# A pair's heads 64 partitions apart: scores as float32 products of two 48-row halves in place of three rounded passes over 96 rows

## The chip, the core and the metric

The kernel runs on one core of a Trainium2 chip. A core has a matrix engine (TensorE, PE in the profile, its weight loads PEld), a vector engine (DVE), a scalar engine (ACT), GpSimd (POOL) and an engine that issues transfers (SyncE, SP). The metric is the device time of one execution in microseconds, the median over the runs shown. Lower is better.

## The reference

Two steps follow each other. First a recurrence over 768 time steps, for 4 batches of 8 heads of 48 features: each head holds a 48 x 48 state.

```
for t in range(S):
    cur = einsum('bhd,bhe->bhde', u * k[t], v[t])
    y[t] = einsum('bhd,bhde->bhe', r[t], state + cur)
    state = w[t][..., None] * state + einsum('bhd,bhe->bhde', k[t], v[t])
```

The outputs of the 8 heads side by side are x, 3072 rows of 384. Then a feed-forward: h = x @ w_in (384 x 2048), g = h * cos(h), out = g @ w_out (2048 x 384). The feed-forward weights arrive as 64-bit floats; all else is float32.

## The kernel before, in words

**Chunks.** Time is cut into chunks of 128 steps, 6 per batch, 24 in all (`j`). Two batches run interleaved, so a chunk's predecessor in its batch is `j` - 2; `c` is the chunk's place in its batch. Inside a chunk the recurrence is written as matrix products. Heads are taken in 4 pairs, 2 x 48 = 96 features on 96 partitions.

**Steps of a chunk.** `load` brings one tile `tt` with r, k and the decays, features on partitions; `lr` and `lv` bring r, k and v with time on partitions. `decay` (L184) makes two running products of the decays by scans (L191, L198; `ee` holds one of them), then multiplies r (`r3`, L203) and k (`k3`, L204) by them in place. `split` (L206) prepares the scores' operands. `a0` and `a1` (L243) make the scores of two pairs each, 128 x 128 per head, into a bank `pa`, and a masked copy (L257) puts the part above the diagonal into `asb`, into which `diag` has put the current step's own term. `t` (L259) transposes k3 into `kn`. `s` (L269) makes the new state `sn` from kn and v; `d` (L235) decays the old state into `dd`. `y` (L296) adds the old state's part (`dd` times `r3`, the past) and the chunk's own (`v` times `asb`) in the bank `py`, heads of a pair in the lower and the upper half of the output's partitions, at 0 and 64. `x` writes the result as high and low parts into `xT`.

**Why a split.** A pair's two heads share the 96 rows of a product, so each head's rows of r must be zero where the other head's lie. The first six chunks (`PLAIN`) do that in float32: r times its decays times a 0/1 column `halves`, twice, on DVE (L211, tile `rzf`). The later 18 also round r and k to a shorter format (f32r) that PE takes in one pass, with the rest as a low part: for each head a masked high part on ACT (L125) and a masked low part on DVE (L219), and a high copy of k on DVE (L130) and its low part on POOL (L133). Three products, high-high, high-low and low-high (L254), then make one pair's scores. A float32 product is one instruction in the program and two rows in the trace; an f32r product is one row.

**Feed-forward.** A block is two chunks, 256 rows. A unit is two 128-wide tiles of the hidden layer: `mm1` is 18 products into `ph` (L363), `gate` (L340 to L344, L130, L133) makes g's high and low parts on ACT, DVE and POOL, and `mm2` is 12 products into `acc` (L377). The 16 weight tiles are made from 64-bit floats during the first part of the program by ACT, DVE and POOL (L125, L155, L156, L158, L130, L133).

**What sets the order.** PE's order is written by hand: `START` up to the point where all weights stand, then `PLAN`, four rows per chunk, with one row for each slot. In these tables `y-1` is the step y of the chunk before, `load+2` the load two chunks ahead; `f` and `w` fetch and convert a weight tile. `NEEDS` and `FREES` add steps that must come first. DVE, ACT, POOL and SP run in the order that a scheduler gives them; `EARLY` and `LATER` choose the engine of a step in the two parts (r3 on DVE early, POOL later; k3 on POOL early, DVE later). `BUFS` gives the number of buffers; `tt` has two. Of PSUM's 8 banks, kind "a" has two in turn while the first two blocks run together, then three, for pa, py, pst (the state's products) and pt (the transposes).

## Time and profile before

| What | Value |
|---|---|
| time, median of 3 runs | 598.83 us (598.5 to 600.02) |
| profiled execution, its span | 597.6 us (the page gives no other time of it) |
| PE busy | 528.2 us, 88% |
| DVE busy | 486.7 us, 81% |
| POOL busy | 333.9 us, 56% |
| ACT busy | 268.6 us, 45% |
| mean granted TensorE clock | 0.977 |

A busy time is the time in which at least one instruction of that engine is under way. Matrix products overlap, so their mean durations are longer than the step from one to the next; the step is read from the starts. A group's line names the source line, the engine, the operation, what it writes and reads, its shapes, the count, the busy time and the mean duration, and then the idle time before it with what ended that.

### The profile page before, as it was taken

What the parts mean: (1) busy time and instruction counts of PE and PEld (TensorE: products, weight loads), DVE (VectorE), ACT (ScalarE), POOL (GpSimd) and SP (SyncE); (2) the same over time, 40 slices, a digit from 0 to 9 for tenths busy, and PEclk for the clock granted to TensorE, in tenths of its full rate; (3) what the DMA queues carried; (4) which work ended last, traced back from release to release, by engine and by line L of the source; (5) the groups of instructions that cost most, each with busy time, mean ns of one, the idle gap of its engine ahead of it and who ended that gap; (6) DMA issues with size and microseconds to landing.
All of it is one profiled execution on the core that took longest, in us unless ns stands there. A gap on an engine that the chain in (4) does not pass through costs nothing.

```text
span 597.6 us, 10845 instructions
## 1 busy us (share of the span) xinstructions
PE 528.2 (88%) x4092; PEld 507.8 (85%) x4092; DVE 486.7 (81%) x839; ACT 268.6 (45%) x476; POOL 333.9 (56%) x338
## 2 busy tenths in 40 slices
PE   1633775979999999999999999999999999999995
PEld 0513674869889999999989999999999999999994
DVE  6998899999997897788899678878877977777641
ACT  2353755643635435544334344444345444434541
POOL 3578496554564566575566456657566554722231
PEclk9999887998999999999999999999999999999998
DMA  8629057022143214214513112331242132055000
GB/s 268 227 97 342 7 167 228 1 67 79 33 129 112 61 54 120 55 41 120 133 33 89 53 47 74 94 95 42 78 120 52 44 93 67 8 185 175 32 1 31
DMA packets 23339, 56.07 MB, mean 94 GB/s; under 512 B 4208, under 2 KB 15088, under 8 KB 23280
## 3 DMA queue, kind: packets, MB, share of 16 engines
q1 hardware_dynamic: 23280, 55.31, 30.7%
q8 instruction: 34, 0.56, 0.4%
q14 instruction: 25, 0.20, 0.1%
HBM read 45.86 MB, written 4.72 MB: 85 GB/s over the span
## 4 chain that ended last, share of the span: by engine, by line
PE 67%; DVE 22%; issue 3%; ACT 3%; POOL 2%; DMA 2%; DVEq 0%; SPq 0%
PE ph L363 27%; PE acc L377 27%; PE py L311 6%; PE pa L254 4%; DVE h L155 2%; DVE h L156 2%; DVE rr L344 2%; DVE rr L341 2%; PE pst L275 2%; DVE ee L191 2%; DMA tt<-tr 2%; POOL h L158 2%; DVE gs L130 1%; DVE tt L198 1%; DVE w L133 1%
## 5 line engine op out<-in xcount | busy, mean ns | idle before, releaser
L133 POOL TENSOR_TENSOR gs<-rr,gs 128x256 fp32r<-128x256 f32 x176 | 166.8, 966 | 188.0 <-DVE gs L130 131.0
L363 PE MATMUL ph<-xT,w 128*128 128x256 f32 x1728 | 225.2, 288 | 28.6 <-DVE xT L130 24.0
L363 PEld LDWEIGHTS ph<-xT,w 128*128 128x128 f32 x1728 | 215.1, 195 | 32.9 <-DVE xT L130 24.8
L377 PE MATMUL acc<-w,gs 128*128 128x384 f32 x1152 | 216.2, 337 | 1.6 <-DVE gs L130 1.2
L377 PEld LDWEIGHTS acc<-w,gs 128*128 128x128 f32 x1152 | 196.3, 188 | 3.5 <-DVE gs L130 1.8
L342 ACT ACTIVATE rr<-rr 128x512 f32<-128x512 f32 x96 | 60.7, 633 | 157.4 <-DVE rr L341 157.3
L344 DVE SCALAR_TENSOR_TENSOR rr<-rr,ph 128x512 f32<-128x512 f32 x96 | 65.2, 679 | 42.5 <-ACT rr L343 42.2
L340 ACT ACTIVATE rr<-ph 128x512 int32<-128x512 f32 x96 | 56.9, 593 | 87.0 <-PE ph L363 80.7
L341 DVE SCALAR_TENSOR_TENSOR rr<-rr,ph 128x512 f32<-128x512 int32 x96 | 65.2, 679 | 26.9 <-ACT rr L340 26.8
L343 ACT ACTIVATE rr<-rr 128x512 f32<-128x512 f32 x96 | 60.6, 632 | 2.7
L158 POOL TENSOR_TENSOR h<-h,rd 128x384 int32<-128x384 int32 x32 | 40.3, 1269 | 27.4 <-DVE h L156 26.9
L130 DVE CAST gs<-rr 128x512 fp32r<-128x512 f32 x96 | 45.1, 470 | 5.8 <-PE acc L377 5.5
L311 PE MATMUL py<-asb,v 128*48 128x128 f32 (+1 forms) x384 | 38.5, 291 | 5.0 <-DVE sn L279 3.8
L233 POOL TENSOR_SCALAR_AFFINE_SELECT asb<-cd 128x512 f32<-128x512 f32 x48 | 33.9, 711 | 7.9 <-DVE cd L230 7.3
L191 DVE TENSOR_TENSOR_SCAN ee<-tt,one_e 96x516 f32<-96x516 f32 x24 | 31.9, 1327 | 6.6 <-DMA tt<-tr 6.5
L198 DVE TENSOR_TENSOR_SCAN tt<-tt,inj 96x516 f32<-96x516 f32 x24 | 36.4, 1517 | 0.5
L257 DVE COPY_PREDICATED asb<-mask,pa 128x512 f32<-128x512 uint8 x48 | 35.1, 735 | 0.9 <-POOL asb L233 0.5
L130 ACT CAST w<-h 128x384 fp32r<-128x384 f32 x32 | 16.4, 514 | 40.9 <-POOL h L158 40.9
L203 POOL TENSOR_TENSOR tt<-tt 96x512 f32<-96x512 f32 x18 | 28.0, 1553 | 9.4 <-DVE tt L198 8.1
L311 PEld LDWEIGHTS py<-asb,v 128*48 128x48 f32 (+1 forms) x384 | 25.7, 139 | 7.3 <-issue 5.7
L254 PE MATMUL pa<-rz,ks 96*128 96x256 f32 x216 | 31.5, 282 | 0.1
L133 POOL TENSOR_TENSOR ks<-tt,ks 96x512 fp32r<-96x512 f32 x18 | 25.9, 1439 | 6.0 <-DVE ks L130 6.0
(69 smaller groups left out, 556.3 us busy)
## 6 DMA issues: line engine op xcount, KB each, us to landing
tt<-tr SPq DMA_DIRECT2D x24, 577.9 KB, 4.7
raw<-wts SPq DMA_DIRECT2D x16, 768.0 KB, 7.2
rk<-tn SPq DMA_DIRECT2D x24, 384.0 KB, 3.7
v<-tn SPq DMA_DIRECT2D x24, 192.0 KB, 2.6
out<-ob SPq DMA_DIRECT2D x24, 192.0 KB, 2.3
ww<-w SPq DMA_DIRECT2D x6, 768.0 KB, 4.6
xf<-yf SPq DMA_DIRECT2D x48, 72.0 KB, 2.6
xf<-yf SPq DMA_DIRECT2D x48, 16.0 KB, 1.9
```

The source lines that it names most:

```text
L130: (nc.scalar.copy if E[name] is nc.scalar else E[name].tensor_copy)(out=out, in_=in_)
L133: E[name].tensor_tensor(out=out, in0=full, in1=high.bitcast(F32), op=ALU.subtract)
L158: nc.gpsimd.tensor_tensor(out=h, in0=h, in1=rd, op=ALU.add)
L254: nc.tensor.matmul(out=pa[:, j], lhsT=a["ks"][:, x, p], rhs=a["rz"][:, y, p].rearrange("p h t -> p (h t)"), start=n == 0, stop=n == 2)
L311: nc.tensor.matmul(out=part[0], lhsT=part[n][0], rhs=part[n][1], start=n == 1 or not part[1], stop=n == 2)
L340: nc.scalar.activation(nn, ph, AF.Copy, scale=INV2PI / W_SCALE)
L341: nc.vector.scalar_tensor_tensor(out=rr, in0=nn, scalar=-2.0 * math.pi * W_SCALE, in1=ph, op0=ALU.mult, op1=ALU.add)
L342: nc.scalar.activation(rr, rr, AF.Sin, scale=0.5 / W_SCALE)
L343: nc.scalar.activation(rr, rr, AF.Square)
L344: nc.vector.scalar_tensor_tensor(out=rr, in0=rr, scalar=-0.5, in1=ph, op0=ALU.add, op1=ALU.mult)
L363: nc.tensor.matmul(out=ph[:, fi], lhsT=wgt[u * FU + fi][:, 0, a, kt * 128:(kt + 1) * 128], rhs=xT[:, b, kt], start=n == 0, stop=n == 3 * K ...
L377: nc.tensor.matmul(out=accs[i][j][:, :DM], lhsT=gs[:, a, fi, j * C:(j + 1) * C], rhs=wgt[u * FU + fi][:, 1, b], start=u == 0 and fi == 0 a ...
```

## The change

Features of a pair's two heads now lie on partitions 0 to 47 and 64 to 111 of `tt`, with the rows between filled (r and k with 0, decays with 1), so all tiles by feature have R = 112 partitions in place of 96, and a load brings 112 rows. A head's rows are then the slice `rows(h)`, and:

- The scores take r3 and k3 directly, in float32, one product per head with 48 rows on each side. The step `split`, the tiles rz, rzf and ks, and the plain kind of chunk are gone. r3 is always multiplied in place by its decays.
- `a0` and `a1` are one step `a`: 8 products, the heads in turn, into two banks, one per head of the pairs. `asb` holds one head of all pairs, four buffers in place of three.
- The state and dd keep each head's own 48 x 48 block alone, so they have half the columns. The state's products are one per head, 48 columns each, in the lower and the upper half of the output's partitions; the state is written by one DVE instruction in place of two masked ones.
- In `y` all of the chunk's own products come first, then the past's, one per head with 48 rows each, where the products before had 96 rows.
- `s` moves from the third row of `PLAN` to the first of the next chunk, beside `y`. `START` has no split, `a0`/`a1` become `a`, and the third chunk's load comes later, since `y` now reads r3 from tt in the first chunks too. `dd` has two buffers. Docstrings go.

```diff
-BUFS = dict(tt=2, rk=2, v=2, h=6, rd=3, rr=7, gs=2, asb=3, ahl=2, sn=2, yf=1, past=2, xT=2, rz=1, kn=2, ee=2, dd=1, xf=6, ks=1, cd=1)
+BUFS = dict(tt=2, rk=2, v=2, h=6, rd=3, rr=7, gs=2, asb=4, ahl=2, sn=2, yf=1, past=2, xT=2, kn=2, ee=2, dd=2, xf=6, cd=1)
...
-PLAN = [["y-1 t mm1 split-1 a0 decay+1 mm2"],
+PLAN = [["y-1 s-1 t mm1 decay+1 mm2"],
         ["lv+1 mm1 mm2 load+2"],
-        ["x-3 a1 mm2 diag+1 s d+1 mm1 lr+3"],
+        ["x-3 a mm2 diag+1 d+1 mm1 lr+3"],
         ["mm1 mm2"]]
-START = ["load0 decay0 t0 lr0 lv0 f load1 decay1 f lr1 d0 split0 load2 f lv1 d1 diag0 a00 f w decay2 s0 f",
+START = ["load0 decay0 t0 lr0 lv0 f load1 decay1 f lr1 d0 lv0 f lv1 d1 diag0 a0 f w decay2 s0 f",
...
-        if not (a["plain"] and FUSE):
-            E["r3"].tensor_tensor(out=a["r3"], in0=a["r3"], in1=a["pp"], op=ALU.mult)
+        E["r3"].tensor_tensor(out=a["r3"], in0=a["r3"], in1=a["pp"], op=ALU.mult)
...
+    def rows(h):
+
+        return slice(ROW * h, ROW * h + HD)
...
+        a["dd"] = dd = buf("dd", [R, NP, HD], F32)
+        E["dd"].tensor_tensor(out=dd, in0=states[a["b"]], in1=a["ee"][:, :, 0:1].to_broadcast([R, NP, HD]), op=ALU.mult)
+
+    def att_scores(a):
+
+        pa = [bank("a", [C, NP, C], "pa") for h in range(2)]
+        for p in range(NP):
+            for h in range(2):
+                nc.tensor.matmul(out=pa[h][:, p], lhsT=a["k3"][rows(h), p], rhs=a["r3"][rows(h), p], start=True, stop=True)
+        for h in range(2):
+            nc.vector.copy_predicated(a["asb", h], mask, pa[h])
...
+    def head_cols(p, h):
+
+        at = p * R96 + h * HD
+        return slice(at, at + (ROW if h == 0 else HD))
...
+        for p in range(NP):
+            for h in range(2):
+                m = ROW if h == 0 else HD
+                at = p * R96 + h * HD
+                nc.tensor.matmul(out=pst[ROW * h:ROW * h + m, p * HD:(p + 1) * HD], lhsT=a["kn"][:, head_cols(p, h)],
+                                 rhs=a["v"][:, at:at + HD], start=True, stop=True)
+        new = pst[:R, :NP * HD].rearrange("p (a e) -> p a e", e=HD)
+        if a["c"] == 0:
+            nc.vector.tensor_copy(out=sn, in_=new)
+        else:
+            nc.vector.tensor_tensor(out=sn, in0=new, in1=a["dd"], op=ALU.add)
...
+        past = a["c"] > 0
         for p in range(NP):
-            parts = []
             for h in range(2):
...
+                m = ROW if h == 0 else HD
+                nc.tensor.matmul(out=py[ROW * h:ROW * h + m, p], lhsT=a["v"][:, head_cols(p, h)], rhs=a["asb", h][:, p],
+                                 start=p == 0, stop=not past, skip_group_check=True)
+        for p in range(NP if past else 0):
+            for h in range(2):
+                nc.tensor.matmul(out=py[rows(h), p], lhsT=a["dd"][rows(h), p], rhs=a["r3"][rows(h), p],
+                                 start=False, stop=True, skip_group_check=True)
```

How the order moves, at three places. First PE in the second part of the program, around a chunk's output: before, the end of y (past and own products in turn), the next chunk's transposes, a unit's first half, and the scores of two pairs.

```order
L311 MATMUL py<-tt,dd 64x128
L311 MATMUL py<-tt,dd 48x128
L311 MATMUL py<-asb,v 64x128
L311 MATMUL py<-asb,v 48x128
L264 MATMUL pt<-ident,tt 128x96 x4
L363 MATMUL ph<-xT,w_987 128x256 x9
L363 MATMUL ph<-xT,w_1055 128x256 x9
L254 MATMUL pa<-rz,ks 128x256 x6
L377 MATMUL acc<-w_480,gs 128x384 x2
```

The same place now, first the end of the state's products and the start of y:

```order
L260 MATMUL pst<-v,kn 48x48
L260 MATMUL pst<-v,kn 64x48
L260 MATMUL pst<-v,kn 48x48
L285 MATMUL py<-asb,v 64x128
L285 MATMUL py<-asb,v 48x128
```

and, three pairs of y later:

```order
L285 MATMUL py<-asb,v 64x128
L285 MATMUL py<-asb,v 48x128
L289 MATMUL py<-tt,dd 48x128 x8
L242 MATMUL pt<-ident,tt 128x112 x4
L342 MATMUL ph<-xT,w_398 128x256 x9
L342 MATMUL ph<-xT,w_433 128x256 x9
L356 MATMUL acc<-w_1211,gs 128x384 x2
```

The state's products (pst) now come straight before the chunk's own products (`asb,v`), the past's (`tt,dd`) follow them in one run of eight, and no scores stand behind this unit.

Second, PE at the scores, once a chunk now, between the second products of two units (`acc`):

```order
L356 MATMUL acc<-w_755,gs 128x384 x2
L356 MATMUL acc<-w_815,gs 128x384 x2
L233 MATMUL pa<-tt 128x128 x8
L356 MATMUL acc<-w_881,gs 128x384 x2
L356 MATMUL acc<-w_941,gs 128x384 x2
```

Eight products of 128 columns stand where twice six of 256 stood, and they read tt alone.

Third, DVE with the first chunk. Before:

```order
L198 SCALAR_TENSOR_TENSOR tt<-tt,inj 96x516
L227 TENSOR_TENSOR rk<-rk 128x384
L228 TENSOR_TENSOR rk<-rk,u_sb 128x384
L230 TENSOR_REDUCE cd<-rk 128x8
L105 TENSOR_REDUCE halves<-ident 96x2
L211 SCALAR_TENSOR_TENSOR rzf<-tt,halves 96x4x128
L98 CAST mask<-maskf 128x512
L211 SCALAR_TENSOR_TENSOR rzf<-tt,halves 96x4x128
L155 TENSOR_SCALAR h<-h 128x384
```

Now:

```order
L197 SCALAR_TENSOR_TENSOR tt<-tt,inj 112x516
L206 TENSOR_TENSOR rk<-rk 128x384
L201 TENSOR_TENSOR tt<-tt 112x512
L207 TENSOR_TENSOR rk<-rk,u_sb 128x384
L209 TENSOR_REDUCE cd<-rk 128x8
L105 TENSOR_REDUCE halves<-ident 96x2
L98 CAST mask<-maskf 128x512
L155 TENSOR_SCALAR h<-h 128x384
```

Two masked products (rzf) are gone and one product of r with its decays (L201) has come in, ahead of the diagonal's work.

More of the change, by code (lines that the diff above doesn't have):

```diff
@@ L22 @@
 R96 = 2 * HD
+ROW = 64
+R = ROW + HD
 NCB = 6
@@ L240, in att_dstate @@
             return
-        a["dd"] = dd = buf("dd", [R96, NP, R96], F32)
-        E["dd"].tensor_tensor(out=dd, in0=states[a["b"]], in1=a["ee"][:, :, 0:1].to_broadcast([R96, NP, R96]),
-                              op=ALU.mult)
-    def att_scores(a, hp):
-        pa = bank("a", [C, 2, 2 * C], "pa")
-        for j in range(2):
-            p = 2 * hp + j
-            if a["plain"]:
-                nc.tensor.matmul(out=pa[:, j], lhsT=a["k3"][:, p], rhs=a["rz"][:, p].rearrange("p h t -> p (h t)"),
-                                 start=True, stop=True)
-                continue
-            for n, (x, y) in enumerate(PASSES):
-                nc.tensor.matmul(out=pa[:, j], lhsT=a["ks"][:, x, p], rhs=a["rz"][:, y, p].rearrange("p h t -> p (h t)"),
-                                 start=n == 0, stop=n == 2)
-        asb = a["asb", hp]
-        nc.vector.copy_predicated(asb, mask, pa.rearrange("p j (h t) -> p (j h) t", h=2))
+        a["dd"] = dd = buf("dd", [R, NP, HD], F32)
[7 more added lines that the diff above has]
+            nc.vector.copy_predicated(a["asb", h], mask, pa[h])
     def att_transpose(a):
@@ L270, in att_state @@
             return
-        sn = buf("sn", [R96, NP, 2, HD], F32)
+        sn = buf("sn", [R, NP, HD], F32)
         pst = bank("a", [C, 512], "pst")
         for p in range(NP):
-            cols = slice(p * R96, (p + 1) * R96)
-            nc.tensor.matmul(out=pst[:R96, cols], lhsT=a["kn"][:, cols], rhs=a["v"][:, cols], start=True, stop=True)
-        new = pst[:R96, :DM].rearrange("p (a h e) -> p a h e", h=2, e=HD)
-        for h in range(2):
-            if a["c"] == 0:
-                nc.vector.tensor_scalar(out=sn[:, :, h], in0=new[:, :, h], scalar1=halves[:, h:h + 1], scalar2=None,
-                                        op0=ALU.mult)
-            else:
-                dd = a["dd"].rearrange("p a (h e) -> p a h e", h=2)
-                nc.vector.scalar_tensor_tensor(out=sn[:, :, h], in0=new[:, :, h], scalar=halves[:, h:h + 1],
-                                               in1=dd[:, :, h], op0=ALU.mult, op1=ALU.add)
-        states[a["b"]] = sn.rearrange("p a h e -> p a (h e)")
+            for h in range(2):
[8 more added lines that the diff above has]
+            nc.vector.tensor_tensor(out=sn, in0=new, in1=a["dd"], op=ALU.add)
+        states[a["b"]] = sn
     def spread(xf, y, h):
@@ L298, in att_out @@
         py = bank("a", [C, NP, C], "py")
+        past = a["c"] > 0
         for p in range(NP):
[L300 removed]
             for h in range(2):
[L302 to L313 removed]
+                m = ROW if h == 0 else HD
+                nc.tensor.matmul(out=py[ROW * h:ROW * h + m, p], lhsT=a["v"][:, head_cols(p, h)], rhs=a["asb", h][:, p],
+                                 start=p == 0, stop=not past, skip_group_check=True)
+        for p in range(NP if past else 0):
+            for h in range(2):
+                nc.tensor.matmul(out=py[rows(h), p], lhsT=a["dd"][rows(h), p], rhs=a["r3"][rows(h), p],
+                                 start=False, stop=True, skip_group_check=True)
+        yf = buf("yf", [R, NP, C], F32)
+        copy("yf", yf, py[:R])
         a["xf"] = buf("xf", [128, KT, C], F32)
         for h in range(2):
[L316 to L318 removed]
+            part = yf[rows(h)]
+            E["qx%d" % h].dma_start(out=a["xf"][h * HD:(h + 1) * HD], in_=part[:, 0:3])
+            spread(a["xf"], part[:, 3], h)
     def att_x(a):
@@ L401, in rwkv_cos_ffn @@
     done = {"f": 0, "w": 0}
-    steps = dict(load=None, lr=att_load_rk, lv=att_load_v, decay=att_decay, split=att_split, diag=att_diag, d=att_dstate,
-                 a0=lambda a: att_scores(a, 0), a1=lambda a: att_scores(a, 1), t=att_transpose, s=att_state, y=att_out, x=att_x)
+    steps = dict(load=None, lr=att_load_rk, lv=att_load_v, decay=att_decay, diag=att_diag, d=att_dstate,
+                 a=att_scores, t=att_transpose, s=att_state, y=att_out, x=att_x)
     def att(j, n):
@@ L491, in rwkv_cos_ffn @@
     nc.tensor.matmul(out=pv[:1, 0:1], lhsT=vote, rhs=ones[:, 0:1], start=True, stop=True)
-    nc.tensor.matmul(out=pv[:1, 1:1 + NP], lhsT=ones[:R96, 0:1], rhs=low, start=True, stop=True)
+    nc.tensor.matmul(out=pv[:1, 1:1 + NP], lhsT=ones[:R, 0:1], rhs=low, start=True, stop=True)
     votes = cst.tile([1, 1], F32, name="votes")
```

81 lines of the change are left out of this document (23 added, 58 removed), and 8 rows, old and new, of the table START.

## The prediction

> **What bounds the kernel now.** I read the page's shares and slices first, then the busy time by stretch, then PE's instructions in order of time inside a full stretch, then DVE's groups inside the start.
>
> ```profile
> PE 528.2 (88%) x4092; PEld 507.8 (85%) x4092; DVE 486.7 (81%) x839; ACT 268.6 (45%) x476; POOL 333.9 (56%) x338
> PE   1633775979999999999999999999999999999995
> DVE  6998899999997897788899678878877977777641
> PE 67%; DVE 22%; issue 3%; ACT 3%; POOL 2%; DMA 2%; DVEq 0%; SPq 0%
> ```
>
> A slice is 15 us. PE reads 9 without a break from the tenth slice on; before that DVE does. Busy time by stretch makes the two stages plain:
>
> ```profile
> 0.00:100.00 100.00, 47.32 (x286) 39.84 (x286) 88.62 (x149) 46.53 (x94) 62.66 (x56) 0.94 0.58 192
> 100.00:180.00 80.00, 71.67 (x490) 67.65 (x491) 78.14 (x130) 37.92 (x71) 45.45 (x41) 0.92 0.24 71
> 180.00:300.00 120.00, 120.00 (x1005) 117.57 (x1004) 100.52 (x177) 54.60 (x92) 70.61 (x73) 1.00 0.30 84
> 300.00:420.00 120.00, 118.91 (x975) 115.38 (x974) 98.51 (x176) 54.25 (x93) 72.27 (x75) 1.00 0.24 69
> ```
>
> The columns after the span are PE, PEld, DVE, ACT, POOL, clock and DMA. Up to 180 us DVE works 166.8 of 180 us and PE is idle for 61.0 (52.7 before 100 us, 8.3 after): this stage waits for DVE. From 180 us PE is busy 120.0 of 120 us and DVE 100.5. There, DVE, ACT or POOL work that goes away buys nothing; only PE work does.
>
> How PE spends that stage shows in its own order of time (start, length, group; what follows starts before the end is drained, so I use differences of starts):
>
> ```profile
> 227.14 0.55 PE L264 MATMUL pt<-ident,tt 96*128 96x96 f32 x4
> 227.47 2.30 PE L363 MATMUL ph<-xT,w 128*128 128x256 f32 x18
> ...
> 237.33 2.25 PE L377 MATMUL acc<-w,gs 128*128 128x384 f32 x12
> 239.42 0.84 PE L275 MATMUL pst<-v,kn 128*96 128x96 f32 x8
> 240.04 4.35 PE L363 MATMUL ph<-xT,w 128*128 128x256 f32 x36
> 244.23 2.25 PE L377 MATMUL acc<-w,gs 128*128 128x384 f32 x12
> 246.41 0.43 PE L311 MATMUL py<-tt,dd 96*64 96x128 f32 x4
> 246.67 0.39 PE L311 MATMUL py<-asb,v 128*48 128x128 f32 x4
> 246.89 0.39 PE L311 MATMUL py<-tt,dd 96*48 96x128 f32 x4
> ...
> 248.31 2.33 PE L363 MATMUL ph<-xT,w 128*128 128x256 f32 x18
> 250.47 0.88 PE L254 MATMUL pa<-rz,ks 96*128 96x256 f32 x6
> 251.19 2.25 PE L377 MATMUL acc<-w,gs 128*128 128x384 f32 x12
> ```
>
> Three prices come out. (1) A float32 product is two rows of the trace. The eight of pst take 240.04 - 239.42 = 0.62 us, 78 ns for 96 columns, so 0.81 ns a column, 103 ns for 128. (2) The py rows step by 0.22 us (246.67 to 246.89) for four rows of 128 columns: 55 ns each, half of 103. The two heads' outputs, in the lower and upper half of the columns, run side by side: 0.11 us a pair. (3) Twelve acc last 2.09 us up to pst but 2.18 up to py, and py takes 1.90 (246.41 to 248.31) for 16 pairs that make 1.76. So going into the split array and out of it costs 0.09 + 0.14 = 0.23 us, about 0.12 an edge; pst, of full width, pays none.
>
> **The change on PE, after 180 us.** How many chunks lie there, from the groups of 180 to 590 us:
>
> ```profile
> L254 PE MATMUL pa<-rz,ks 96*128 96x256 f32 x207 | 30.3, 281 | 0.0
> L311 PE MATMUL py<-tt,dd 96*64 96x128 f32 x128 | 25.2, 278 | 0.0
> L275 PE MATMUL pst<-v,kn 128*96 128x96 f32 x112 | 11.7, 247 | 0.0
> L264 PE MATMUL pt<-ident,tt 96*128 96x96 f32 x52 | 7.1, 260 | 0.0
> ```
>
> By 12, 8, 8 and 4 rows a chunk: 17 chunks of scores (the last rows of 207 are of the edge), 16 with a past, 14 states, 13 transposes.
>
> Scores. Before: 2 x 0.72 us (250.47 to 251.19) = 1.44. After: 8 float32 products of 48 rows by 128 columns, 16 rows of the trace. The trace shows no product on half the rows. Lower bound: the halves pair as the column halves do, 8 x 0.11 + 0.23 for two edges = 1.11. Upper bound: one after another, 16 x 0.103 + 0.23 = 1.88. I take 1.11, by the nearest row, py's pairs: -0.33 x 17 = **-5.6 us** (upper end +0.44 x 17 = +7.5). Between them lies a limit by weight loads: each half loads 128 columns, and four pt, which load 128 each, take 0.33 us, so a load fits into 83 ns; two in turn make 166 a pair, 8 x 0.166 + 0.23 = 1.56, +2.0 us in all. The Trainium skill, TensorEngine Tiling (Array Packing), section Tiling Modes, says that different tiles can load weights and multiply in parallel; by that rule the scores would cost 1.11 and not 1.56 a chunk, 7.6 us less in all, and no row here shows row tiles.
>
> Past. Before, 8 pairs of it sit among the asb pairs; now 8 pairs of 48 rows follow them. The pairs cost the same 0.88 us; new is one edge between the asb products (all rows) and these (half the rows): 0.12 x 16 = **+1.9**. If they run one after another: 16 x 0.103 - 0.88 = +0.77 a chunk, +12.3 more.
>
> State. Before 0.62. After 16 rows of 48 columns, straight ahead of the asb products and in the same column halves, so no further edge. Lower bound by columns, 8 x 48 x 0.81 ns = 0.31; upper, py's full pair, 0.88. I take 0.55, the middle, since neither row is nearer: -0.07 x 14 = **-1.0** (-4.3 to +3.6). Transposes move 112 columns for 96: 0.33 x 112/96, +0.05 x 13 = **+0.7**.
>
> Sum on PE: -5.6 + 1.9 - 1.0 + 0.7 = **-4.0 us**. PE's order moves the state from before the next unit to just ahead of py, and merges the scores; between scores and py lie over 8 us of units, and DVE, with less to do, has the two masked copies ready long before.
>
> **The change on DVE, before 180 us.** Its groups in that stretch:
>
> ```profile
> L211 DVE SCALAR_TENSOR_TENSOR rzf<-tt,halves 96x512 f32<-96x512 f32 x12 | 10.0, 837 | 0.0
> L242 DVE TENSOR_TENSOR dd<-sn,ee 96x384 f32<-96x384 f32 x4 | 4.5, 1115 | 0.0
> L283 DVE SCALAR_TENSOR_TENSOR sn<-pst,halves,dd 96x192 f32<-96x192 f32 x8 | 3.0, 405 | 0.0
> L219 DVE SCALAR_TENSOR_TENSOR rz<-tt,halves,rz 96x512 fp32r<-96x512 f32 x2 | 2.2, 1116 | 0.0
> L279 DVE TENSOR_SCALAR sn<-pst,halves 96x192 f32<-96x192 f32 x4 | 1.5, 400 | 0.0
> L204 DVE TENSOR_TENSOR tt<-tt,ee 96x512 f32<-96x512 f32 x2 | 1.4, 678 | 0.0
> L130 DVE CAST ks<-tt 96x512 fp32r<-96x512 f32 x1 | 0.4, 417 | 0.0
> ```
>
> Gone: rzf 10.0, rz 2.2, ks 0.4, half the state's writes (4.5 / 2) and half of dd (4.5 / 2): 17.1. New: r3 times the decays for the first six chunks, at L204's 0.678: 4.1. Net 13.0 us less. This stage has 61 us of idle PE, so most should come through. Not all: after 100 us PE has only 8.3 us left to give, and one load waits longer:
>
> ```profile
> 19.40 0.33 SPq L173 DMA_DIRECT2D tt<-tr  x1
> ```
>
> ```profile
> 17.36 1.97 PE L250 MATMUL pa<-rzf,tt 96*128 96x256 f32 x4
> 21.50 1.95 PE L311 MATMUL py<-asb,v 128*64 128x128 f32 x16 [2.17 <-DVE sn L279]
> ```
>
> The third tt was issued at 19.4 us, once the first chunk's scores had read theirs. Now y needs r3 from tt too, so it goes out after py, by these rows about 23.4: 4 us later, with a raw weight and the first xf transfers behind it on SP. DVE's order now has two tiles' weight conversions ahead of that chunk's scan, which covers it; without that cover it costs 4. The first tt also grows; the chain of waits begins with it:
>
> ```profile
> 0.81 4.93 DMA tt<-tr
> ```
>
> It is on the chain for 4.93 us and grows by 112/96: at most +0.8, I take +0.5. What the split took from ACT and POOL, and from DVE after 180 us, counts nothing, covered by PE's full time. I take two thirds of 13.0, **-8.7 us**, between 0 and -13.
>
> **Sum.** -8.7 + 0.5 - 4.0 = -12.2 against the span of 597.6: 585.4. The median, 598.83, lies 1.2 above that span, as what the span leaves out at both ends and the scatter of 598.5 to 600.02. Carried over: **586.6 us**, own range 580 to 592.
>
> **The rivals.**
> - *The halves do not run at once* (the change then doesn't do what it says). Scores +7.5, past 1.9 + 12.3, state and transposes -0.3: +21.4 on PE, -8.2 at the start, so 612 us. For: no row shows half the rows in use. Against: py's 55 ns on half the columns. It decides once a chunk costs PE 0.72 us (12.2 / 17) more than in my sum. Slower. 0.12.
> - *Only the past products are serial*, since both halves write the same bank of py: -5.6 + 14.2 - 0.3 = +8.3, -8.2: 598.9, no change. Against: py's column halves write one bank at 55 ns a row. 0.07. The Trainium skill's same page, Restrictions and Gotchas, says that row tiles cannot access one PSUM bank simultaneously; by that rule the time would be this case's 598.9 and not 586.6.
> - *Weight loads limit the scores*: +2.0 in place of -5.6, the sum on PE +3.6: 594.2. For: pt's 83 ns a load; against: py loads 112 columns in 110 ns, no faster than pt, so a rate for 256 isn't shown. 0.13.
> - *The start keeps its length*, the held load and the conversions' POOL and ACT steps taking DVE's place: only -4.0 + 0.5, 595.3. For: POOL works 62.7 of the first 100 us; against: DVE's 88.6. 0.13.
> - The forecast: 0.55.
>
> **How the numbers follow.** The range of 578 to 601 holds the forecast, the two middling cases and the even one, and leaves out the first rival and a little of the low end. Within 0.3% of 598.83, about what a measurement of this kernel can tell from no change, is 597.0 to 600.6. Faster: nearly all of 0.55, most of 0.13 + 0.13, a part of 0.07: 0.76. Within: 0.08. Slower: 0.12 and the high ends of the others: 0.16.
>
> **What would show it.** A score group of 16 rows in about 1.1 us between two acc groups, its rows in pairs; 1.65 or more shows the first rival, 1.3 and more weight loads. The past's 16 rows in about 0.9 to 1.0. PE full from about 170 us instead of 180, with DVE busy about 154 us by then. ACT and POOL lose the split's work with nothing gained by it after 180 us. Wrong altogether would be PE with new idle time after 180 us (waiting for dd, whose state now comes almost a chunk later, or for tt), or a start as long as before.

## The result and the profile after

The changed kernel took 604.01 us (median, 603.12 to 604.24) against 599.12 us (598.5 to 600.02) on the same chip: a ratio of 1.0078, 95% interval 1.0061 to 1.0094. It is slower by 4.9 us, where 12.2 us less were forecast. Its profiled execution took 603.12 us, 601.4 of it the span.

The page of the changed kernel: busy shares, two lines of the slices, and the chain that ended last.

```profile
PE 524.5 (87%) x4372; PEld 496.4 (83%) x4372; DVE 446.1 (74%) x759; ACT 245.2 (41%) x440; POOL 268.2 (45%) x320
...
PE   2513744998998999999999999999999999999995
...
DVE  6989899998765785786696758858957865767641
...
PE 66%; DVE 19%; DMA 6%; issue 4%; POOL 3%; ACT 1%; SPq 0%; DVEq 0%; POOLq 0%
```

DVE sheds 40.6 us in all, and its line shows it from the tenth slice on. PE's line is full from about the same slice as before, with an 8 at the tenth and the thirteenth, and weaker at the sixth and seventh (44 for 75). The same stretches as in the prediction:

```profile
0.00:100.00 100.00, 43.94 (x348) 38.49 (x348) 87.82 (x143) 48.91 (x99) 61.86 (x58) 0.91 0.57 193
100.00:180.00 80.00, 69.83 (x528) 66.15 (x528) 67.66 (x121) 33.40 (x64) 38.90 (x39) 0.90 0.28 84
180.00:300.00 120.00, 117.82 (x1020) 111.86 (x1021) 85.68 (x149) 46.55 (x79) 50.14 (x64) 0.97 0.28 82
300.00:420.00 120.00, 119.66 (x1059) 113.76 (x1058) 89.57 (x158) 45.90 (x79) 51.26 (x68) 1.00 0.27 77
```

Before 180 us DVE is busy 155.5 us (87.82 + 67.66) where it was 166.8: 11.3 less, near the 13.0 forecast. Yet PE is busy 113.8 us in place of 119.0, so it has done less.

The two traced executions differ by 3.8 us. Where these come from is read from one landmark: the start of the tenth unit's first products (the 325th row of ph), ahead of which PE has the same steps in both kernels. It stood at 187.3 us and stands at 192.2: **+4.9**. From there to the 46th of the 48 units, with the same work in both (1,296 rows of ph, 852 of acc, 17 score groups), it was 371.2 us and is 370.1: **-1.1**. The rest is 39.1 us in both. So the start lost 4.9 where it was to win 8.2, and the full stage won 1.1 where it was to win 4.0.

**The full stage.** PE in order of time in the changed kernel, around one score group and one chunk's state and y (start, length, group):

```profile
197.79 0.86 PE L356 MATMUL acc<-w,gs 128*128 128x384 f32 x4
198.57 1.16 PE L233 MATMUL pa<-tt 48*128 48x128 f32 x16
199.67 2.36 PE L356 MATMUL acc<-w,gs 128*128 128x384 f32 x12
...
250.40 0.61 PE L260 MATMUL pst<-v,kn 128*64 128x48 f32 x15
...
250.90 1.05 PE L285 MATMUL py<-asb,v 128*64 128x128 f32 x15
251.88 1.08 PE L289 MATMUL py<-tt,dd 48*48 48x128 f32 x16
252.89 2.33 PE L342 MATMUL ph<-xT,w 128*128 128x256 f32 x18
```

The scores take 199.67 - 198.57 = 1.10 us, the past's 16 rows 1.01, the state 0.50 (its last rows and the first of y alternate at 250.8): the halves do run at once. I summed the differences of starts over the two equal stretches, by kind of row: scores -5.1 us, y +1.4 (the new edge ahead of the past is in it, 202 ns a chunk), state -1.2, transposes +0.5, changes from one group to the next +0.3. That is -4.1, the forecast's -4.0 almost to the tenth. Three things that the forecast had not named gave back 3.0: ph rows +1.2, acc rows +1.4, waits +0.4.

**The start.** What PE waited for between 54 and 187 us (in total, times, longest; the first line of each kernel also holds the wait that ends at 54 us, 16.8 us before and 21.6 after, which begins earlier). Before:

```profile
PE ph L363 <- DVE xT L130: 23.7, 2, 16.8
PE pt L264 <- DVE asb L257: 4.0, 1, 4.0
PE pst L275 <- DVE asb L257: 3.3, 1, 3.3
...
PE pa L250 <- ACT kn L130: 1.1, 1, 1.1
```

After:

```profile
PE ph L342 <- DVE xT L130: 31.2, 3, 21.6
PE pst L260 <- DVE asb L235: 6.4, 2, 5.3
PE pa L233 <- ACT kn L130: 3.5, 1, 3.5
PE pa L233 <- DVE sn L266: 2.6, 1, 2.6
PE pt L242 <- DVE asb L235: 2.3, 1, 2.3
```

The waits of 5.3 and 3.5 us are both chunk 3's. PE there, before:

```profile
75.84 1.06 PE L250 MATMUL pa<-rzf,tt 96*128 96x256 f32 x4
77.98 1.13 PE L250 MATMUL pa<-rzf,tt 96*128 96x256 f32 x4 [1.09 <-ACT kn L130]
79.14 0.92 PE L275 MATMUL pst<-v,kn 128*96 128x96 f32 x8
81.97 0.69 PE L311 MATMUL py<-rzf,dd 96*64 96x128 f32 x4 [1.92 <-DVE asb L257]
...
85.53 2.33 PE L363 MATMUL ph<-xT,w 128*128 128x256 f32 x18
```

And after, with DVE's two rows behind the scores:

```profile
73.49 0.49 PE L233 MATMUL pa<-tt 48*128 48x128 f32 x2
77.49 2.07 PE L233 MATMUL pa<-tt 48*128 48x128 f32 x14 [3.52 <-ACT kn L130]
84.87 0.98 PE L260 MATMUL pst<-v,kn 128*64 128x48 f32 x15 [5.31 <-DVE asb L235]
...
89.39 2.39 PE L342 MATMUL ph<-xT,w 128*128 128x256 f32 x18
```

```profile
83.23 0.95 DVE L133 TENSOR_TENSOR gs<-rr,gs 128x256 fp32r<-128x256 f32 x1
84.10 1.34 DVE L235 COPY_PREDICATED asb<-mask,pa 128x512 f32<-128x512 uint8 x2
86.01 0.36 DVE L266 TENSOR_TENSOR sn<-pst,dd 112x192 f32<-112x192 f32 x1 [0.58 <-PE pst L260]
```

In this stage two blocks run together and kind a has two banks. Before, the scores were two steps of two pairs each, one bank a step, and the state could take the first bank as soon as its masked copy was through, while the second was still worked on. Now one step takes both banks, and since the heads alternate in it, both are complete only at its end. It waits for the second bank in its middle (77.49) and ends at about 79.6. DVE, which is busy all the while, reaches the two copies in its order only at 84.10, and the state waits until it has made one: of the wait of 5.3 us, 4.5 lie between the scores' end and the copies' turn on DVE. Chunk 3's y ends, and the next unit starts, 89.39 - 85.53 = 3.9 us later. The unit that waits for this chunk's x starts 3.9 later too (98.9 and 102.8).

That lag does not simply run on to the tenth unit's 4.9. At the sixth unit it is down to 0.1 (135.2 and 135.3), since the kernel before waits there for chunk 4's copy (the 3.3 above). At the seventh it is 3.5 again (145.5 and 149.0): the merged scores of chunk 5 wait 2.6 us for the bank of chunk 4's state (the row with sn above), once more a step that needs both banks.

### The profile page after: what moved, and what is told of

Same layout as the page of the kernel before. It is cut to its first block, busy times and chain, and to the rows that moved or that the text cites. A ratio compares the mean times of both kernels' runs of the same rounds, so it can differ in the third digit from the quotient of the medians.

```text
span 601.4 us, 11254 instructions
## 1 busy us (share of the span) xinstructions
PE 524.5 (87%) x4372; PEld 496.4 (83%) x4372; DVE 446.1 (74%) x759; ACT 245.2 (41%) x440; POOL 268.2 (45%) x320
## 4 chain that ended last, share of the span: by engine, by line
PE 66%; DVE 19%; DMA 6%; issue 4%; POOL 3%; ACT 1%; SPq 0%; DVEq 0%; POOLq 0%
PE ph L342 29%; PE acc L356 26%; DMA tt<-tr 6%; PE py L285 3%; PE py L289 3%; PE pa L233 3%; POOL h L158 2%; DVE h L156 2%; DVE h L155 2%; DVE shrink L193 2%; PE pst L260 2%; DVE xT L133 2%; DVE rr L320 1%; DVE w L133 1%; PE pt L242 1%
## 5 line engine op out<-in xcount | busy, mean ns | idle before, releaser
L133 POOL TENSOR_TENSOR gs<-rr,gs 128x256 fp32r<-128x256 f32 x176 | 137.7, 801 | 168.5 <-DVE gs L130 152.9
L158 POOL TENSOR_TENSOR h<-h,rd 128x384 int32<-128x384 int32 x32 | 41.2, 1293 | 22.9 <-DVE h L156 20.1
L190 DVE TENSOR_TENSOR_SCAN ee<-tt,one_e 112x516 f32<-112x516 f32 x24 | 30.8, 1283 | 27.7 <-DMA tt<-tr 27.6
L130 DVE CAST gs<-rr 128x512 fp32r<-128x512 f32 x96 | 41.6, 433 | 6.9 <-PE acc L356 6.8
L233 PE MATMUL pa<-tt 48*128 48x128 f32 x384 | 34.1, 310 | 8.0 <-ACT kn L130 3.8
L233 PEld LDWEIGHTS pa<-tt 48*128 48x128 f32 x384 | 28.1, 208 | 14.8 <-ACT kn L130 4.3
L201 POOL TENSOR_TENSOR tt<-tt 112x512 f32<-112x512 f32 x18 | 21.5, 1193 | 35.3 <-DVE tt L197 35.3
L226 POOL TENSOR_TENSOR dd<-sn,ee 112x192 f32<-112x192 f32 x16 | 9.6, 601 | 61.9 <-DVE ee L190 52.1
L235 DVE COPY_PREDICATED asb<-mask,pa 128x512 f32<-128x512 uint8 x48 | 32.5, 725 | 0.0
L285 PE MATMUL py<-asb,v 128*48 128x128 f32 (+1 forms) x384 | 30.1, 294 | 1.1 <-DVE asb L235 1.1
L197 DVE TENSOR_TENSOR_SCAN tt<-tt,inj 112x516 f32<-112x516 f32 x24 | 30.8, 1285 | 0.2
```

The source lines that it names most:

```text
L130: (nc.scalar.copy if E[name] is nc.scalar else E[name].tensor_copy)(out=out, in_=in_)
L133: E[name].tensor_tensor(out=out, in0=full, in1=high.bitcast(F32), op=ALU.subtract)
L158: nc.gpsimd.tensor_tensor(out=h, in0=h, in1=rd, op=ALU.add)
L233: nc.tensor.matmul(out=pa[h][:, p], lhsT=a["k3"][rows(h), p], rhs=a["r3"][rows(h), p], start=True, stop=True)
L285: nc.tensor.matmul(out=py[ROW * h:ROW * h + m, p], lhsT=a["v"][:, head_cols(p, h)], rhs=a["asb", h][:, p], start=p == 0, stop=not past, sk ...
```

## Experiments

Three theories of the start, told apart by the first eight runs. A: tt is released later, and DVE waits for its load. B: the scores hold both banks. C: DVE's busy time never set the start's length, so that shedding it buys nothing. All times are medians, and the ratios are to the kernel before on the same chip, which gave 599.4 to 600.0 throughout. One reservation holds for all: in the start only PE's order is by hand, and the scheduler plans the other engines' order anew for nearly every edit.

**One more tt buffer (A).**

```diff
-BUFS = dict(tt=2, ...
+BUFS = dict(tt=3, ...
```

> The change with three buffers of tt in place of two, so that a load no longer waits for y of two chunks before. Theory A (late load: y now holds tt in the start too, DVE stands in order at the decay scan until the tile lands, and xT stands behind it; DVE waited 27.6 us for tt loads, 6.5 before): the start regains 4 to 9 us and the later stage 1 to 3, 593 to 599 us against the change's 604.0, and DVE's wait for tt falls under 8 us. Theory B (both banks: in the first stage the scores take both banks of kind a at once, so PE's next step waits for both masked copies): only the later stage's 1 to 3 us, 601 to 603. Theory C (the weight conversions through ACT and POOL set the start's length whatever DVE sheds): 601 to 604.

605.8 us (604.91 to 606.22), ratio 1.0104 [1.0087, 1.0121]: nothing won.

**The two heads' scores as two steps, one bank each (B).** For the first six chunks, at the two places that they had in the program before.

```diff
+    def att_head(a, h):
+        pa = bank("a", [C, NP, C], "pa")
+        for p in range(NP):
+            nc.tensor.matmul(out=pa[:, p], lhsT=a["k3"][rows(h), p], rhs=a["r3"][rows(h), p], start=True, stop=True)
+        nc.vector.copy_predicated(a["asb", h], mask, pa)
...
-         "w w a2 d2 f w t2 f mm1 w s2 y2 d3 mm1 f x2 mm2 f f diag3 t3 f a3 w f load4 s3",
+         "w w b2 c2 d2 f w t2 f mm1 w s2 y2 d3 mm1 f x2 mm2 f f diag3 t3 f b3 c3 w f load4 s3",
```

> The change with the first six chunks' scores as two steps, head 0 and head 1, each into one bank, at the places in START where the kernel before had its two half steps; later chunks as in the change. Theory B: the waits of PE for a masked copy ahead of the state's products (10.9 us in all) go, and PE reaches the same unit 4 to 6 us sooner, 597 to 600. Theory A: 602 to 605. Theory C: 602 to 605.

596.86 us (596.17 to 599.76), ratio 0.9947 [0.993, 0.9963]: 7.1 us less than the changed kernel (7.9 by the two ratios), and faster than the kernel before. The trace is of the slowest of the five executions, 599.76. PE at chunk 3 in this kernel, and DVE's two copies:

```profile
71.55 1.16 PE L241 MATMUL pa<-tt 48*128 48x128 f32 x8
76.95 2.08 PE L241 MATMUL pa<-tt 48*128 48x128 f32 x8 [4.25 <-ACT kn L130]
78.96 1.09 PE L267 MATMUL pst<-v,kn 128*64 128x48 f32 x16
82.10 1.97 PE L292 MATMUL py<-asb,v 128*64 128x128 f32 x16 [2.05 <-DVE asb L242]
84.00 1.95 PE L296 MATMUL py<-tt,dd 48*48 48x128 f32 x16
85.87 4.21 PE L349 MATMUL ph<-xT,w 128*128 128x256 f32 x18
```

```profile
77.60 0.72 DVE L242 COPY_PREDICATED asb<-mask,pa 128x512 f32<-128x512 uint8 x1
...
81.32 0.72 DVE L242 COPY_PREDICATED asb<-mask,pa 128x512 f32<-128x512 uint8 x1
```

The state follows the scores at once (78.96), y is done 3.5 us earlier than in the changed kernel, and the tenth unit starts at 186.3 in place of 192.2. B holds: the loss at the start comes from the merged step. The wait of 4.25 us for the transposes' bank stays.

**Both (A and B).** The two edits above together.

> Both edits together. If A and B each hold in part: under 597 us. If C holds: 600 to 604, the later stage's waits alone regained. The forecast of the start (8.7 us less than before) would need about 588.

600.78 us (598.51 to 601.76), ratio 1.0019 [1.0004, 1.0034]: the buffer took the split's gain away again. What in it cost this I did not find: the two traces differ by 0.5 us only (598.5 and 598.0), the split kernel's being of its slowest execution.

**The halves one after another, within the one step.**

```diff
-        for p in range(NP):
-            for h in range(2):
+        for h in range(2):
+            for p in range(NP):
```

> The change with the scores of all pairs' first heads issued ahead of all second heads, so that neighbours in the order use the same half of the rows. If the halves run at once only when they alternate in the order: 16 x 0.103 + 0.23 = 1.88 us a chunk in place of 1.09, +0.79 x 17 = +13 us in the later stage, about 617. If PE pairs them over a longer stretch of the order: no change, 603 to 605.

605.44 us (603.58 to 606.16), ratio 1.0085 [1.0063, 1.0108]. The total looks like no change, and both of its halves moved. A score group in the full stage:

```profile
194.12 1.71 PE L233 MATMUL pa<-tt 48*128 48x128 f32 x16
195.76 2.36 PE L356 MATMUL acc<-w,gs 128*128 128x384 f32 x12
```

It takes 1.64 us for 1.10: products of one half in a row mostly no longer pair (three of the 16 rows still start within 6 ns of another, where the two heads meet), and it is the interleaved order that pairs them. From the tenth unit on this costs 7.6 us. But the tenth unit starts at 187.6, 4.6 earlier: head 0's bank is complete while head 1's products still run, its copy goes ahead (at 78.5 in place of 84.1), and in place of the wait of 5.3 us stands one of 2.1.

This is B a second time, by another edit, and it narrows B down. Here too one step takes both banks, yet the loss at chunk 3 is gone; so what costs there is not that both are taken at once but that neither is complete, and neither copy can go ahead, before the whole step is done. (At chunk 5, where the step waits for the state's bank, a wait of 2.0 us stays.) One thing the two edits don't separate: in both, the scheduler's order on DVE differs from the changed kernel's from the 22nd row on. How much of the loss lies in the bank itself, and how much in the late place that the scheduler gave the copies, stays open.

**Extra tt and v buffers with the split (A).** Since v's load stands ahead of tt's on SP's queue, one buffer alone might not have freed tt.

```diff
-BUFS = dict(tt=2, rk=2, v=2, ...
+BUFS = dict(tt=3, rk=2, v=3, ...
```

> The two-step scores of the first chunks (596.9 us) with three buffers of tt and three of v: on SP v's load stands ahead of tt's and itself waited for y (about 225 us of SP's time in both the change and the run with three tt), so the third tt alone moved nothing. Theory A (the load's lateness costs): with both gone tt goes out before y, DVE's wait for tt (29.0 us) falls under 5 us, PE's idle 2.6 us near 175 us and the small ones after it go, 3 to 5 us less: 592 to 594. Rival (the waits were cover for nothing, since PE is full after 180 us): 596 to 598.

599.76 us (598.57 to 601.83), ratio 1.0006 [0.9991, 1.002]: no gain. DVE's wait for tt over the whole execution (total, times, longest), in the changed kernel, and then in this one:

```profile
DVE ee L190 <- DMA tt<-tr: 27.6, 17, 3.5
```

```profile
DVE ee L190 <- DMA tt<-tr: 29.9, 17, 3.7
```

The wait is 27.6 us where it was 6.5 before the change, and it does not shrink with the buffers: SyncE, which issues the loads in order, still stands 205.7 us at v's load waiting for py (228.9 in the changed kernel). So this run did not take the wait away, and says nothing on what it costs. What speaks against A as the cause of the loss is the split kernel: it has the same wait, 29.0 us, and its tenth unit starts 5.9 us sooner. In the start the wait comes to 4.6 us in the changed kernel (1.9 at 158 us, 2.7 at 177) besides the first load's 3.5, and the second of these stands ahead of a wait of PE for xT of 2.8; the kernel before has neither. Whether that part of the relief was lost there stays open.

**The state back at its former place in the plan, with the split.**

```diff
-PLAN = [["y-1 s-1 t mm1 decay+1 mm2"],
+PLAN = [["y-1 t mm1 decay+1 mm2"],
...
-        ["x-3 a mm2 diag+1 d+1 mm1 lr+3"],
+        ["x-3 a mm2 diag+1 s d+1 mm1 lr+3"],
```

> The two-step scores with the state's step back in the third row of the plan, where the kernel before has it, so that its products stand alone between a unit's products. By the edges of 0.12 us: two more a chunk, 14 x 0.23 = +3.2 us, 600. By the step of the first products (ph took 113 ns each behind a float32 group and 118 behind acc, and 594 of them stood behind a float32 group in the kernel before, 90 in the change): 36 x 4.5 ns x 14 = -2.3 us, so about +0.9 in sum, 597.8.

597.09 us (595.65 to 599.47), ratio 0.9961 [0.9946, 0.9976]: the same as the split alone. The state's own edges come back, and more groups of ph follow a float32 group.

**x sooner: ACT's order by hand in the start, with the split.**

```diff
-BY_HAND = "P"
+BY_HAND = "PA"
...
-         "c0 y0 diag1 b1 x0 t1 f w lr2 s1 diag2 lv2 w c1 y1 load3 x1 mm1 lr3 lv3 decay3",
+         "c0 y0 diag1 b1 x0 t1 f w lr2 s1 diag2 lv2 c1 y1 w load3 x1 mm1 lr3 lv3 decay3",
```

> The two-step scores with ACT's order in the first part by hand and the third weight tile's conversion behind the second chunk's output, so that on ACT the copy of py (yf) stands ahead of the casts of weight tiles which wait for POOL. In the trace of the two-step run the second py ended at 33 us, its copy ran at 41.7 behind such casts, and the first unit's products began at 53.1. Theory C (ACT's and POOL's queues set the first 54 us, not DVE's work): the first unit begins 5 to 10 us sooner; the whole gains up to that where DVE keeps up, 588 to 595. Rival (DVE's work sets it): the first unit begins where it did and the sum stays, 596 to 600.

638.88 us (638.22 to 640.73), ratio 1.0663 [1.0641, 1.0684]. The first ph did start 8.7 us earlier, at 44.4 in place of 53.1. Then PE's waits between 30 and 230 us in this kernel read:

```profile
PE ph L349 <- DVE xT L130: 21.9, 3, 12.2
PE ph L349 <- DVE rr L330: 19.6, 7, 4.4
PE pst L267 <- ACT kn L130: 16.2, 1, 16.2
```

An order by hand that is good for y's copy puts kn and the gates behind the weight conversions on ACT. The run says nothing on an earlier x by itself; it shows what a queue in order costs.

**The kernel before with less work on DVE (C).**

```diff
-            for h in range(2):
+            for h in range(1):
...
-        E["ru"].tensor_tensor(out=rk, in0=rk, in1=u_sb, op=ALU.mult)
```

> The kernel before with DVE work left out and nothing else moved by hand: one of each chunk's two masked copies of r in the first six chunks (6 x 0.837 = 5.0 us; both heads then use the first head's copy) and the product of r, k and u without u (9 x 0.72 = 6.5 us before 180 us). Output differs in those parts. The forecast's step (a DVE second less before 180 us is two thirds of a second off the time): 11.5 us less work, 7.7 us off, about 591. Theory C (queues and waits set the start): 0 to 3 us off, 596 to 599.

598.79 us (597.58 to 601.47), ratio 0.999 [0.9976, 1.0004]. Its first two stretches:

```profile
0.00:100.00 100.00, 49.30 (x289) 41.45 (x290) 86.98 (x146) 46.14 (x94) 59.08 (x57) 0.92 0.61 198
100.00:180.00 80.00, 72.73 (x495) 69.13 (x495) 70.24 (x120) 36.79 (x70) 44.79 (x41) 0.89 0.22 66
```

DVE works 157.2 us before 180 us, 9.6 less than before, nearly the change's 11.3, and without its banks, tiles and buffers. The tenth unit starts at 186.7 in place of 187.3. So a relief that by the forecast's two thirds was to bring 6.4 us brings about 0.6. The split kernel says the same: DVE works 157.5 us there, and the tenth unit starts 1.0 earlier than before. C holds as to what shedding DVE's time buys, with the reservation above.

Where the relief went shows in the chain that ended last, followed back by the profile. Of the first 187 us it spends 114.6 in DVE's rows in the kernel before, so DVE was on it most of the time; with less DVE work it spends 89.6 there. But its time in POOL's rows goes from 14.3 to 24.3 us (the sums of the weight tiles, L158, from 9.3 to 21.1) and in loads from 4.9 to 13.8. What DVE gave up, POOL's conversions and the loads took.

**The granted clock (D).** The traces raised one more suspect. After idle times of PE of some 2 us and more the granted clock is mostly 0.50 for a while, and a ph row then takes 213 ns in place of 113 to 118. Up to the tenth unit PE was busy 19.5 us at half clock before the change, 28.2 after it, 25.8 in the split kernel (the expectations below have 18.4, 27.9 and 25.1). If that counted in full, half of the extra 8.7 us, 4.4, would be most of the 4.9. I filled PE's idle times with throw-away products into unused columns of an accumulator's bank:

```diff
+    def busy(n):
+        for _ in range(n):
+            nc.tensor.matmul(out=accs[0][0][:, 384:512], lhsT=ident, rhs=ident, start=False, stop=False, skip_group_check=True)
...
-         "w w b2 c2 d2 f w t2 f mm1 w s2 y2 d3 mm1 f x2 mm2 f f diag3 t3 f b3 c3 w f load4 s3",
-         "y3 f x3 mm1 mm2 mm2 ...
+         "w w b2 c2 d2 f w t2 f mm1 w s2 y2 d3 mm1 f x2 mm2 f f diag3 t3 f b3 z36 c3 w f load4 s3",
+         "z14 y3 f x3 mm1 mm2 mm2 ...
...
+            busy(FILL.get(up1[0], 0))
             mm1(up1[0])
```

(z36 stands for 36 of them.)

> The kernel with the first six chunks' scores as two steps (596.86 us), plus throw-away products of TensorE, identity by identity into unused columns of the accumulator's bank, at the places where TensorE stood idle before 190 us: 36 between the two heads' scores of chunk 3, 14 before its y, 30, 20 and 20 before the ph groups of units 5, 13 and 17. Theory D (the granted clock): in that kernel 30.7 us before 190 us ran at half the granted clock, each stretch beginning at an idle time of 2 us or more, and TensorE worked 25.1 us in them at 213 ns a product in place of 117. With the idle times filled the stretches shrink to 10 us or less, and of the 25.1 us up to 17 are worked at full rate: up to 7.8 us less, some of which turns into waits: 590 to 594 us. Rival (TensorE waits for the other engines' results in this stage, whatever its clock): the stretches shrink as well, but the idle time grows by what the products save, and the time stays at 596 to 598.5 us.

617.3 us (615.75 to 620.82), ratio 1.031 [1.0287, 1.0334]. In the changed kernel, likewise:

> The changed kernel (604.01 us) itself, plus the same throw-away products at its own idle times: 28 and 20 inside the scores of chunks 3 and 5, 44 before chunk 3's state, 54 and 24 before the ph groups of units 5 and 17. In it 41.0 us before 190 us ran at half the granted clock, with 27.9 us of TensorE's work in them, against 23.9 and 18.4 us before the change. Theory D: the stretches fall to 14 us or less, and 20 us of work at the full rate give up to 9 us: 596 to 600 us, so the clock carried the larger part of the change's loss at the start. Rival: the waits alone made the loss, 602.5 to 605 us.

624.48 us (623.34 to 625.32), ratio 1.0416 [1.04, 1.0432]. PE's work at half clock fell to 11.8 and 6.8 us, but the products were twice as long as I had reckoned and held back what stood behind them. Then with fewer of them:

> As the split kernel with filled idle times, but with the number of throw-away products cut to fit: the first try showed that one identity product takes two passes of 115 ns, so that 120 of them took 27.7 us where 13 to 16 us of idle time had been meant, and held the work behind them back. Now 15 between the two heads' scores of chunk 3 (3.5 us in an idle time of 4.25), 6 before its y (1.4 in 2.05), 13, 8 and 9 before the ph groups of units 5, 13 and 17 (3.0 in 3.65, 1.8 in 2.5, 2.1 in 2.6). Theory D (the granted clock): TensorE's work at half clock before 190 us falls from 25.1 us to 12 or less, which is worth 5 to 6 us where TensorE is the one that is waited for: 591.5 to 595.5 us. Rival (TensorE waits for the other engines here, whatever its clock): 596 to 599 us, with idle time and fillers together longer than the split kernel's idle time by what the clock saved.

> The changed kernel (604.01 us) with throw-away products cut to fit its own idle times: 12 and 8 inside the scores of chunks 3 and 5 (2.8 us in an idle time of 3.52, 1.8 in 2.6), 18 before chunk 3's state (4.1 in 5.31), 24 and 10 before the ph groups of units 5 and 17 (5.5 in 6.81, 2.3 in 2.81). Theory D: TensorE's work at half clock before 190 us falls from 27.9 us to 14 or less, worth up to 6 us: 598 to 601.5 us. Rival: 602.5 to 605.5 us.

604.9 us (603.23 to 605.26), ratio 1.0095 [1.0078, 1.0112], and 607.74 (605.07 to 608.95), 1.0132 [1.01, 1.0164]. Half clock took 10.2 and 10.3 us of PE's work in place of 25.8 and 28.2, and both kernels were slower than without. In the first of them chunk 3's y began at 84.5 in place of 82.1, but its x reached PE at 102.3 in place of 98.0: the scheduler, which sees the products, had given DVE, ACT and POOL another order there. So these four do not separate clock and order. The next three were built so that the other engines keep their order (32 columns a product, which the scheduler reckons as short), or all but keep the work and change the order (48 columns):

> The split kernel (596.86 us) with throw-away products of 32 columns at three idle times of TensorE: 24 between the two heads' scores of chunk 3, 11 before its y, 20 before the ph group of unit 5. The order on DVE, ACT, POOL and SP stays row for row that of the split kernel. Between 60 and 112 us the split kernel had 20.5 us at half clock with 16.8 us of TensorE's work in them. Theory D (the granted clock): of these at most 7 us stay, worth up to 4.5 us, of which two thirds arrive: 592.5 to 595 us. Rival (the others' results set this stage, whatever TensorE's clock): the half clock goes, and the time stays at 596 to 598.5 us.

> The same 55 products as in the run with the unchanged order, but of 48 columns in place of 32, which is enough for the scheduler to order DVE's instructions otherwise from its 115th row on, ACT's from the 78th, POOL's from the 48th. TensorE's added work differs by less than 1 us. Theory F (the scheduler's order moves the start by several us whatever the edit): 3 us or more away from the run with the unchanged order, most likely 600 to 605 us as in the other kernel with fillers and a new order (604.9). Rival: within 1.5 us of the run with the unchanged order.

> The changed kernel (604.01 us) with throw-away products of 32 columns at three of its idle times: 18 within chunk 3's scores, 28 before its state, 36 before the ph group of unit 5; the order on DVE, ACT, POOL and SP stays row for row that of the changed kernel. Between 60 and 112 us it had 27 us at half clock with 15.7 us of TensorE's work in them. Theory D: at most 7 us of that work stay at half clock, worth up to 4 us: 600 to 602.5 us. Rival: 603.5 to 605 us.

603.8 us (600.41 to 607.34), ratio 1.0072 [1.0045, 1.0098]; 603.61 (602.34 to 605.23), 1.0072 [1.0056, 1.0088]; 613.89 (611.3 to 614.15), 1.0236 [1.0221, 1.0251]. The first two are equal within their scatter, so the other order alone, at that place, moved nothing that shows. But none of the three answers D. Two stretches of the first (span, PE, PEld, DVE, ACT, POOL, clock):

```profile
74.00:79.00 5.00, 5.00 (x46) 4.88 (x44) 5.00 (x9) 3.71 (x9) 3.90 (x5) 1.00 0.62 200
79.00:96.00 17.00, 17.00 (x104) 15.84 (x104) 10.12 (x19) 7.27 (x16) 8.11 (x8) 0.50 0.26 87
```

PE is busy without a gap, and the clock is halved all the same, 4.5 us after the products of 32 columns begin (74.46): they do not keep it up. They also took as long as those of 128, 112 ns a pass and 213 at half clock, so that they overran the idle times. Chunk 3's y ended 6.5 us later than in the split kernel (92.4 and 85.9), the tenth unit started 3.5 later: in this stage PE's step for a chunk counts, through y, the transfers and x.

The last: 64 columns, fewer, fitted to the idle times, the order kept.

> The split kernel (596.86 us) with throw-away products of 64 columns, by 115 ns a pass and two passes each: 14 between the two heads' scores of chunk 3 (3.2 us in an idle time of 4.25), 5 before its y (1.15 in 2.05), 9 before the ph group of unit 5 (2.1 in 3.65). The order on DVE, ACT, POOL and SP stays that of the split kernel. Theory D (the granted clock): the half clock from 76.5 to 90.1 us, with 12 us of TensorE's work in it, goes or shrinks to one quantum of 3.4 us; chunk 3's y, 3.9 us in the split kernel, takes 2.1; chunk 3's x and all after it come 2 to 4 us earlier: 593 to 595.5 us. Rival (this stage waits for the other engines' results): the half clock goes and the time stays, 596 to 598 us. If the half clock stays although TensorE is busy, the run says nothing on this, and the fillers cost 2 to 6 us.

598.24 us (596.76 to 600.94), ratio 0.9977 [0.9963, 0.9991]; by the medians not faster than the split kernel. (In the traces its tenth unit starts 1.6 us earlier, at 184.7, but the split kernel's trace is of its slowest execution.) PE in it:

```profile
74.91 3.34 PE L380 MATMUL acc<-ident 128*128 128x64 f32 x28
78.17 1.16 PE L242 MATMUL pa<-tt 48*128 48x128 f32 x8
79.26 0.67 PE L268 MATMUL pst<-v,kn 128*64 128x48 f32 x16
79.85 1.33 PE L380 MATMUL acc<-ident 128*128 128x64 f32 x10
82.79 1.09 PE L293 MATMUL py<-asb,v 128*64 128x128 f32 x16 [1.61 <-DVE asb L243]
```

The scores and the state at chunk 3 run at the full rate (1.09 and 0.59 us in place of 2.01 and about 1.0), and y starts at 82.8 all the same, as in the split kernel at 82.1: there it waits for DVE's copy, whatever PE's clock. Half-clock work fell from 25.8 to 18.9 us only: the clock is halved again from 83.8 to 90.6, through the past and the next unit. So the clock is shown not to set when chunk 3's y starts; what it costs elsewhere in the start stays open. By its median, none of the filled kernels was faster than the same kernel without fillers.

That the clock is not the loss of 4.9 us follows from runs without fillers. The split kernel has 6.3 us more work at half clock than the kernel before, and its tenth unit starts 1.0 earlier. The kernel with the halves one after another has 30.0 us of it, more than the changed kernel's 28.2, and starts 4.6 earlier than that.

## Why the prediction was wrong

- *Scores at 1.11 us a chunk*: right, 1.10, in pairs. The Trainium skill, TensorEngine Tiling (Array Packing), section Tiling Modes, has different tiles load and multiply in parallel; the trace agrees, with 1.10 and not the 1.56 of loads in turn. With one half's products in a row it was 1.64.
- *Past +1.9, state -1.0, transposes +0.7*: +1.4, -1.2, +0.5. Right. (The state's 0.55 us is called the middle of 0.31 and 0.88, which is 0.60; with that the term is -0.3. It measured 0.50.) The rival in which only the past is serial is out: both halves of it write one bank, and its 16 rows take 1.01 us. The Trainium skill, TensorEngine Tiling (Array Packing), section Restrictions and Gotchas, would have row tiles not share a bank at once; these tiles, in different rows and columns, did, and the measurement decides.
- *The sum on PE, -4.0*: its terms came to -4.1 and the stage won 1.1. Missing were three small terms. Rows of ph step by 113 ns behind a float32 group and by 117 to 118 behind acc; the merged scores and the moved state leave fewer float32 groups in front of ph (+1.2). The first acc product behind a score group takes 284 ns in place of 173, so a second part of the edge shows one row later (17 x 0.11 = 1.9, +1.4 net on acc). Waits, 0.4.
- *"Net 13.0 us less. This stage has 61 us of idle PE, so most should come through"*: **this is the step that failed.** The term of -8.7 us has a relief behind it that came (11.3 us for 13.0) and brought next to nothing: a like relief of 9.6 in the kernel before moved the tenth unit by 0.6, and with the scores in two steps the change moved it by 1.0. A busy share of 89% in the first 100 us was read as the bound, and PE's idle time as time that DVE alone kept empty. The runs show in its place that others stand right behind DVE: with less DVE work the chain that ended last passes through POOL's rows (24.3 us for 14.3) and loads (13.8 for 4.9).
- *"DVE, with less to do, has the two masked copies ready long before"*: true after 180 us, where over 8 us of units lie between scores and y. I carried it over to the start without looking. There the state follows the scores directly, the merged step completes neither bank before its end, and DVE gets to the copies 4.5 us after that. This made the sign: undoing it alone is worth 7.1 us in the medians, 5.9 at the tenth unit of the traces.
- *The third tt, 4 us later and covered*: wrong, though it cost nothing. The third load went out at 13.88 us, right behind the first chunk's scores and 5.5 earlier than before (19.40): the first chunk of a batch has no past, so its y reads no r3 and holds no tt. The later third load that the section on the change speaks of did not come about, for the same reason. The waits for tt that grew, from 6.5 to 27.6 us, are those of later chunks.
- *The first tt, +0.5*: not seen. The first scan started at 5.6 us in place of 5.8.
- *The start keeps its length (595.3)* was the rival nearest in mechanism, at 0.13, and POOL's part in its reason is borne out by the chain. It was still on the wrong side: no rival had the start grow. The range of 578 to 601 ended 3 us short, since each of its ends took the start's change between 0 and -13.

## What to carry to other kernels

Merging two steps that each take a buffer of a small pool changes when the first buffer is complete and how long the pool is held: list, in each stage, who takes the next buffer, which release it waits for, and where that release stands in its engine's order, before pricing the instructions. Neither an engine's busy share nor its part in the chain that ended last prices a relief of it: ask what the chain would run through next, and leave the work out of the kernel before as a first experiment. And pairs of products on two halves of the array pair only when they are issued in turn.

## What the runs showed of the hardware

- A float32 product with a 128 by 128 weight takes two passes of 112 ns whether 32, 48, 64 or 128 columns go through, and of 213 ns at half clock. That the weight load sets this step is argued from the columns making no difference. The Trainium skill, TensorE: Matmul & The Clock Gate, section LDWEIGHTS (loading the stationary operand), has a weight load take its columns divided by 1.2 in ns, 107 here. These products come near it, but the transposes of the kernel before, which load 128 columns each, follow one another by 83 ns.
- The granted clock fell to 0.50 about idle times of PE of mostly 1.9 us and more, in some runs of 1.2 to 1.6, and also, with no idle time, after 4.5 us of products of 32 or 48 columns; with 64 and 128 columns at the same place it stayed at 1.00. The Trainium skill, TensorE: Matmul & The Clock Gate, section The HAM clock gate, has a gate that sets the clock by how busy the array was in a window of about 3.4 us. The stretches at half clock here are multiples of 3.4 us, which agrees, and by these runs an array that is occupied is not always busy enough.
- Passing between products on the whole array and on half of it costs at each edge: from acc into a split group 268 ns in place of 174, out of it 200 to 202, and once more 284 for the first acc row that follows it.
